# An attention and two feed-forward layers on one core: part of the first feed-forward block done inside the attention, in half units, with PSUM divided anew and a TensorE turn between the layers

## The chip, the cores and the metric

The kernel runs on one core of a Trainium2 chip. A core has TensorE (PE in the rows; PEld is its weight load), VectorE (DVE), ScalarE (ACT), GpSimd (POOL), SyncE (SP, which only issues transfers here) and 16 DMA engines. The metric is the device time of one execution in microseconds; smaller is better.

## The reference

Inputs are float32. Three layers follow each other:

```python
B, H, S, D = 2, 8, 576, 64                      # attention
q_rot, k_rot = (rotate(q), rotate(k))           # rotary position coding
scores = scale * np.matmul(q_rot, k_rot.transpose(0, 1, 3, 2))
scores = scores - np.max(scores, axis=-1, keepdims=True)
attn = np.exp(scores)
attn = attn / (np.sum(attn, axis=-1, keepdims=True) + 1e-09)
x = np.matmul(attn, v)                          # then to [1152 tokens, 512]

p = domain_probs / (domain_probs.sum(-1, keepdims=True) + 1e-09)
for e in range(4):                              # first feed-forward layer
    h = np.maximum(x @ w1[e], 0.0)              # 512 -> 1024
    out += p[:, e:e + 1] * (h @ w2[e])          # 1024 -> 512

h = out @ w_in                                  # second layer, 512 -> 2048
g = np.maximum(0.01 * h, h)
return g @ w_out                                # 2048 -> 512
```

## The kernel before

**Precision.** Each matmul operand is split into a rounded part and a rest ("hi" and "lo"), and three products (hi·lo, hi·hi, lo·hi) are summed in PSUM. For the weights POOL makes hi (L480) and lo (L484); for the hidden values ACT makes hi from PSUM (L531) and DVE lo (L535).

**Attention.** The 16 heads are worked on in pairs: pairs p = 0 to 3 belong to the first batch of 576 tokens, 4 to 7 to the second. For each pair x (q and k with their rotated partners) is loaded, rope is done by multiplications and an addition (L192, L195), hi and lo are made, and the halves are stacked into stk by transfers. A pair has nine score tiles: eight of 128 queries of one head (s, L275, four matmuls of 288 columns) and one for the 64 left queries of both heads. Each goes through DVE's maximum (L292), ACT's exponential (L302), transposes on PE (t, L348 and L354), hi on ACT (L373) and lo on DVE (L377). Two groups of queries (c = 0 with 320, c = 1 with 256) then give four sums over v (o, L430, in v_sum), whose two halves are added by ACT and DVE (L395, L400), and are multiplied by the reciprocals of the row sums, which two groups of transposes (rb, L332) spread over the partitions. x_out writes hi and lo into xT, the input of the next layer, turned, with tokens along the free axis. The PSUM of this part: ps_s two tiles of two banks, ps_t three banks for t and rb, ps_o one bank for o.

**Feed-forward.** xT has three blocks of tokens (512, 384, 256), xT0 to xT2. Block 0 holds tokens of the first batch only. The hidden columns are cut into 12 units of 512: units 0 to 7 are the four experts, two each, units 8 to 11 the second layer. For each unit u and block b stage 1 makes four tiles ph (L524, 12 matmuls each, relu or the leaky form on the way out), stage 2 one tile py (L430, 12 matmuls) for every 128 tokens, which DVE adds to acc (L567 to L574). Weights are transferred and split one unit ahead. The second layer's weights come as 64-bit values whose conversion (L495 to L513) uses DVE, POOL and ACT. Stage 1 of unit 0 on block 0 ("fill") is planned into the end of the attention, three matmuls at a time, and its weights are split there too.

**The turn between the layers.** After unit 7 acc, with tokens on the partitions, becomes the xT of the second layer. DVE transposes 32x32 blocks of an acc tile (L585), a transfer writes the tile of 256 KB to a DRAM buffer td (L590), four strided transfers read it back turned into xs (L599), ACT makes hi (L602) and DVE lo (L606). There are nine tiles.

**Order.** Nothing is ordered at run time. Plan is a list scheduler that runs when the program is built: each task has an engine or several to choose from, a length, what it comes after, and a rank; the task that can start earliest, and of those the one with the smallest rank, is put next on its engine. RANK and MORE hold the rank offsets of the attention's tasks, MORE what a second choice of engine adds. Ring stands for the rotation of a pool's buffers: a new tile comes after the users of the tile whose buffer it gets. There are two plans, one for the attention and one for the feed-forward part. On the chip each engine runs its list in order.

Of the kernel before, what the change touches and what calls it, by code (L numbers as in the profile page):

```python
# [20 lines left out]
P = 128  # L21
# [5 lines left out]
FU = 512  # L27
WARM = 22

RANK = {"tab_q": 1616.7, "zero": 1714.1, "load_x1": 1343.2, "load_x0": 2035.5, "rope01": 1752.5, "rope11": 2011.1, "rope21": 2017.5, "rope00": 2016.3,  # L30
        "rope10": 2000.0, "rope20": 1286.4, "x_hi1": 1338.5, "x_lo1": 1797.8, "x_hi0": 1168.4, "x_lo0": 1247.5, "stack1": 1313.2, "stack0": 1342.0,
        "diag": 1829.6, "load_v": 2038.3, "v_hi": 1678.4, "v_lo": 1951.8, "first_diag": 1240.7, "first_q": 1338.7, "scores": 1176.7, "max": 1822.3,
        "exp": 2029.1, "turn": 1666.7, "t_hi": 1805.0, "t_lo": 1825.5, "v_sum": 2012.8, "v_copy": 1150.2, "v_add": 1277.5, "r_add": 1843.8, "r_inv":
        1936.1, "r_rows": 1790.6, "r_wide": 1760.7, "x_mul": 1431.7, "x_out_hi": 2033.4, "x_out_lo": 2016.2, "load_w": 1702.3, "split_w": 1791.5,
        "fill0": 1333.5, "fill1": 2064.3, "fill2": 2004.3, "fill3": 1161.5, "fill_hi": 2024.3, "fill_lo": 1243.1}
# [14 lines left out]
LAG = {"PE": 0.2, "ACT": 0.16, "DVE": 0.19, "POOL": 0.1, "SP": 0.65, "DMA": 2.2}  # L50


class Plan:
# [17 lines left out]
    def order(self):  # L71
# [10 lines left out]
        while len(order) < len(self.tasks):  # L82
            best = None
            for e, items in ready.items():
# [7 lines left out]
            _, _, i, us = min((x for x in ready[e] if x[0] <= t), key=lambda x: x[0] if e == "DMA" else x[1:3])  # L92
# [35 lines left out]
def attention_then_two_ffns(ctx, tc, xqk, vp, rope, dprob, w1, w2, w_in, w_out, out):  # L128
# [8 lines left out]
    w1a_p = ctx.enter_context(tc.tile_pool(name="w1a", bufs=1))  # L137
    ha_p = ctx.enter_context(tc.tile_pool(name="ha", bufs=1))
# [25 lines left out]
    x_p, hl_p, stk_p, v_p, vs_p = opened("x", 2), opened("hl", 1), opened("stk", 2), opened("v", 1), opened("vs", 2)  # L164
    p_p, pl_p, st_p, pt_p = opened("p", 2), opened("pl", 2), opened("st", 4), opened("pt", 1)
    xo_p, tab_p, sm_p = opened("xo", 1), opened("tab", 1), opened("sm", 2)
    ps_s, ps_t, ps_o = (opened(n, b, space=PSUM) for n, b in (("ps_s", 2), ("ps_t", 3), ("ps_o", 1)))
# [159 lines left out]
    def r_rows(p, c):  # L327


        RB[p, c] = ps_t.tile([P, 3 - c, P], F32, tag="t", name=f"rb{p}_{c}")  # L330
        for j in range(2):
            pe.transpose(RB[p, c][:, j], RW[p, c][:, j].rearrange("p h d -> p (h d)"), ident)  # L332
        if c == 0:
            pe.transpose(RB[p, c][:, 2], SM[p][:, 4:5].to_broadcast([P, P]), ident)

    def t_turn(p, i, u):
# [6 lines left out]
        if i < KT:  # L343
            t = ps_t.tile([P, 3, P], F32, tag="t", name=f"t{p}_{i}_{u}")
# [4 lines left out]
        else:  # L349
            t = ps_t.tile([P, KT + 1, KR], F32, tag="t", name=f"t{p}_{i}_{u}")  # L350
# [28 lines left out]
    def v_sum(p, h, c):  # L379
        pt, vs = PT[p, c], VS[p]  # L380
        o = PO[p, h, c] = ps_o.tile([P, sum(k for _, k in RUNS[c])], F32, tag="o", name=f"o{p}_{h}_{c}")
# [54 lines left out]
    SEQ = [(u, b) for u in range(NU) for b in range(3)]  # L436
# [150 lines left out]
    def turn_out(blk, i):  # L587
        t = BLOCKS[blk][0] // P + i
        td = td_p.tile([P, DM], F32, tag="td", name=f"td{t}")
        sp.dma_start(td, TURN[blk, i])  # L590
        TURN[blk, i] = td

    def turn_in(blk, i, q):
        t = BLOCKS[blk][0] // P + i
        if q == 0:
            TURN["x", blk, i] = xs_p.tile([P, NC, P], F32, tag="xs", name=f"xs{t}")

        src = TURN[blk, i].rearrange("(a j) (c q i) -> q j c a i", a=4, c=NC, q=4)
        sp.dma_start(TURN["x", blk, i][32 * q:32 * q + 32].rearrange("j c (a i) -> j c a i", a=4), src[q])  # L599

    def turn_hi(blk, i):
        act.activation(xT[blk][:, 0, :, i * P:(i + 1) * P], TURN["x", blk, i], AF.Copy)  # L602

    def turn_lo(blk, i):
        s = slice(i * P, (i + 1) * P)
        dve.tensor_tensor(out=xT[blk][:, 1, :, s], in0=TURN["x", blk, i], in1=f32(xT[blk][:, 0, :, s]), op=ALU.subtract)  # L606


    with tc.manual_schedule():

        t = ps_o.tile([P, P], F32, tag="o", name="warm")
        for _ in range(WARM):
# [3 lines left out]
        rings = {k: Ring(v) for k, v in {"xk": 2, "xq": 2, "hl": 1, "stk": 2, "v": 1, "vs": 2, "p": 2, "pl": 2, "s": 2, "t": 3,  # L616
                                         "pt0": 1, "pt1": 1, "o": 1, "xf0": 1, "xf1": 1, "sm": 2, "rw": 2}.items()}
# [15 lines left out]
        def transfer(kind, n, fn, kb, after):  # L633
            return dma(fn, kb, after, n + RANK[kind], 0.48 if "load" in kind else 0.65)
# [14 lines left out]
        for p in range(NP_ALL):  # L649
# [52 lines left out]
            muls = []  # L702
            sm_t, sm_w = fresh("sm")
            for n in range(n0, n0 + PER):
# [21 lines left out]
                for u in ([1, 2] if h else [0]) if big else [0, 1]:  # L726
                    t_t, t_w = fresh("t")
# [3 lines left out]
                    for k in range(1 if big else 2):  # L731
# [3 lines left out]
                        rings["t"].use(t_t, lo)  # L735
                        for g in [0, 1] if big and u == 1 else [u // (1 + big)]:
                            written.setdefault((g, c), []).append(lo)
                if (i, h) in ((1, 1), (KT - 1, 1)):
# [3 lines left out]
                    for g in range(2):  # L742
                        o_t, o_w = fresh("o")
# [6 lines left out]
                        rings["o"].use(o_t, adds[-1])  # L750
# [199 lines left out]
```

## Time and profile before

| | us |
|---|---|
| median of 3 runs (lowest, highest) | 810.25 (809.1, 812.9) |
| the profiled execution | 808.0 |
| its span | 806.1 |
| PE busy | 756.7 (94%) |
| PEld busy | 666.8 (83%) |
| DVE busy | 429.3 (53%) |
| POOL busy | 379.0 (47%) |
| ACT busy | 293.1 (36%) |

The span is the time from the first to the last instruction of the profiled execution. The busy times are sums over a program with parts of very different character, the attention up to about 190 us, the feed-forward layers behind it, with the turn at about 570 to 618 us, so what bounds the kernel is read part by part.

### The profile page before, as it was taken

The page shows a single profiled execution, that of the slowest core. Times are in us where ns is not written, and L with a number is a line of the kernel's source. Part 1 is how long each engine was busy: PE and PEld are TensorE (multiplying, and loading weights), DVE is VectorE, ACT ScalarE, POOL GpSimd, SP SyncE. Part 2 cuts the span into 40 slices and gives each one's busy share as a digit, 9 for nine tenths or more (in the row PEclk, how much of TensorE's full clock was granted, in tenths as well). Part 3 has the DMA queues.
Part 4 walks back from the last instruction along what each step waited for, and adds up shares of the span by engine and source line. Part 5 has one row for each costly group of instructions (what it writes and reads, how often), then busy time and mean ns, then how long its engine had stood idle before and what let it go on. Part 6 is the DMA issues. An engine that isn't in the chain of part 4 may idle for free.

```text
span 806.1 us, 11011 instructions
## 1 busy us (share of the span) xinstructions
PE 756.7 (94%) x4160; PEld 666.8 (83%) x4160; DVE 429.3 (53%) x691; ACT 293.1 (36%) x666; POOL 379.0 (47%) x395
## 2 busy tenths in 40 slices
PE   6888888899999999999999999999956999999998
PEld 6777777788988888888888888889745889888897
DVE  7879999884132222222224222378785388773222
ACT  3878888772011011101112011224354445552221
POOL 7777777625903321333313333145374368673221
PEclk9999999999999999999999999999978999999999
DMA  7566665540401101111003111032774031000011
GB/s 227 140 180 173 160 168 156 121 178 27 157 26 53 48 14 45 52 53 53 27 27 104 53 53 32 22 105 79 168 210 92 1 104 53 1 1 1 0 53 66
DMA packets 47348, 66.13 MB, mean 82 GB/s; under 512 B 22848, under 2 KB 24640, under 8 KB 47296
## 3 DMA queue, kind: packets, MB, share of 16 engines
q1 hardware_dynamic: 47296, 65.44, 28.0%
q8 instruction: 33, 0.54, 0.3%
q14 instruction: 19, 0.16, 0.1%
HBM read 48.32 MB, written 4.72 MB: 66 GB/s over the span
## 4 chain that ended last, share of the span: by engine, by line
PE 79%; DVE 12%; ACT 3%; DMA 2%; issue 1%; POOL 1%; SPq 1%; DVEq 0%; ACTq 0%; POOLq 0%
PE ph L524 36%; PE py L430 33%; PE s L275 4%; PE o L430 4%; DVE pt L377 3%; DVE nm L292 3%; PE t L348 1%; DVE bd L288 1%; DVE xf L400 1%; ACT p L302 1%; ACT pt L373 1%; DMA raw<-in_w_in_dram 1%; DMA tab<-in_rope_dram 1%; DMA xs<-td 1%; SPq L599 1%
## 5 line engine op out<-in xcount | busy, mean ns | idle before, releaser
L524 PE MATMUL ph<-xT,w 128*128 128x256 f32 (+2 forms) x1728 | 308.7, 337 | 9.9 <-DVE xT L606 9.9
L524 PEld LDWEIGHTS ph<-xT,w 128*128 128x128 f32 x1728 | 281.0, 190 | 35.1 <-DVE xT L606 10.3
L430 PE MATMUL py<-w,h 128*128 128x512 f32 (+1 forms) x1308 | 302.7, 389 | 6.6 <-ACT h L547 5.5
L430 PEld LDWEIGHTS py<-w,h 128*128 128x128 f32 x1308 | 243.5, 188 | 57.4 <-ACT h L547 6.2
L531 ACT ACTIVATE h<-ph 128x512 fp32r<-128x512 f32 (+2 forms) x96 | 46.8, 492 | 305.3 <-PE ph L524 289.1
L480 POOL TENSOR_SCALAR w<-raw 128x512 fp32r<-128x512 f32 x64 | 40.0, 648 | 187.4 <-PE py L430 99.2
L535 DVE SCALAR_TENSOR_TENSOR h<-ph,h 128x512 fp32r<-128x512 f32 (+2 forms) x96 | 53.1, 557 | 127.7 <-ACT h L531 127.7
L570 DVE SCALAR_TENSOR_TENSOR acc<-py,prob,acc 128x512 f32<-128x512 f32 x63 | 47.1, 747 | 94.4 <-PE py L430 94.4
L549 POOL TENSOR_TENSOR h<-g,h 128x512 fp32r<-128x512 f32 (+2 forms) x48 | 51.5, 1073 | 77.3 <-ACT h L547 48.3
L484 POOL TENSOR_TENSOR w<-raw,w 128x512 fp32r<-128x512 f32 x64 | 81.5, 1299 | 0.0
L513 POOL TENSOR_TENSOR w<-t,w 128x512 fp32r<-128x512 f32 x32 | 44.1, 1392 | 48.8 <-ACT w L510 48.8
L275 PE MATMUL s<-stk 128*128 128x288 f32 x288 | 54.4, 323 | 12.4 <-ACT p L302 8.3
L504 POOL TENSOR_TENSOR t<-t,r 128x512 int32<-128x512 int32 x32 | 45.0, 1407 | 34.9 <-DVE t L497 24.1
L377 DVE TENSOR_TENSOR pt<-t,pt 128x384 fp32r<-128x384 f32 (+2 forms) x128 | 58.1, 489 | 2.3 <-ACT pt L373 1.2
L275 PEld LDWEIGHTS s<-stk 128*128 128x128 f32 x288 | 43.3, 201 | 16.5 <-ACT p L302 11.2
L373 ACT ACTIVATE pt<-t 128x384 fp32r<-128x384 f32 (+2 forms) x128 | 52.3, 440 | 11.5 <-PE t L348 10.0
L292 DVE TENSOR_REDUCE nm<-s 128x1 f32<-128x576 f32 x72 | 53.8, 753 | 4.7 <-PE s L275 3.9
L302 ACT ACTIVATE p<-s,nm 128x576 f32<-128x576 f32 x72 | 53.3, 741 | 5.2 <-DVE nm L292 4.7
L430 PE MATMUL o<-pt,vs 128*128 128x320 f32 (+1 forms) x256 | 46.3, 306 | 6.0 <-DVE xf L400 5.7
L348 PE MATMUL t<-ident,p 128*128 128x128 f32 x288 | 44.6, 283 | 3.1 <-DVE pt L377 2.5
L545 DVE TENSOR_TENSOR g<-ph,g 128x512 f32<-128x512 f32 (+2 forms) x48 | 26.5, 553 | 37.2 <-ACT g L543 37.0
L543 ACT ACTIVATE g<-ph 128x512 f32<-128x512 f32 (+2 forms) x48 | 23.4, 488 | 62.1 <-PE ph L524 59.4
(80 smaller groups left out, 644.3 us busy)
## 6 DMA issues: line engine op xcount, KB each, us to landing
raw<-in_w_dram SPq DMA_DIRECT2D x32, 512.0 KB, 3.7
raw<-in_w_in_dram SPq DMA_DIRECT2D x16, 512.0 KB, 4.1
raw<-in_w_out_dram SPq DMA_DIRECT2D x16, 512.0 KB, 3.7
x<-in_xqk_dram SPq DMA_DIRECT2D x14, 576.0 KB, 5.3
stk<-hl SPq DMA_DIRECT2D x28, 288.0 KB, 4.8
stk<-hl SPq DMA_DIRECT2D x28, 144.0 KB, 2.5
v<-in_vp_dram SPq DMA_DIRECT2D x8, 288.0 KB, 4.7
td<-tr SPq DMA_DIRECT2D x9, 256.0 KB, 2.5
```

Of the source, the lines that this page charges most:

```text
L275: pe.matmul(sc[:, c, :HS], lhsT=l, rhs=r[:, c * HS:(c + 1) * HS], start=(k == 0), stop=(k == len(ops) - 1))
L292: dve.tensor_reduce(out=NM[n], in_=SC[n][:, :, :HS], axis=AX.XY, op=ALU.max, negate=True)
L302: act.activation(PP[p, i][:, h].rearrange("p (c k) -> p c k", c=2), SC[n][:, :, :HS], AF.Exp, bias=NM[n], accum_out=SM[p][:, col:col + 1])
L348: pe.transpose(t[:, j], flat[:, b * P:(b + 1) * P], ident)
L373: act.activation(hi, src, AF.Copy)
L377: dve.tensor_tensor(out=lo, in0=src, in1=f32(hi), op=ALU.subtract)
L430: pe.matmul(ps, lhsT=l, rhs=r, start=(k == 0), stop=(k == len(ops) - 1))
L484: pool.tensor_tensor(out=w[:, 1], in0=raw, in1=f32(w[:, 0]), op=ALU.subtract)
L524: pe.matmul(ps, lhsT=w[:, c, l, fs], rhs=x[:, r, c], start=(c, k) == (0, 0), stop=(c, k) == (NC - 1, 2))
L535: dve.scalar_tensor_tensor(out=lo, in0=ps, scalar=0.0, in1=f32(hi), op0=ALU.max, op1=ALU.subtract)
L549: pool.tensor_tensor(out=lo, in0=g, in1=f32(hi), op=ALU.subtract)
L570: dve.scalar_tensor_tensor(out=acc, in0=ps, scalar=prob[:, t, e:e + 1], in1=acc, op0=ALU.mult, op1=ALU.add)
```

## The change

**Half units in the attention.** Block 0 of units 0 to 2 is taken out of the feed-forward order (`SEQ`) and done inside the attention's plan, after block 0 of xT is complete, that is, after pairs 0 to 3. Each unit is cut into two half units v of 256 hidden columns: two transfers of 512 KB (half_load), four hi splits on POOL or ACT and four lo splits on POOL, two tiles hp of 12 matmuls with their relu on ACT and DVE, and four tiles hy of six matmuls that DVE adds to acc. Units 0 to 2 still run on blocks 1 and 2 in the second plan, and transfer and split their weights again. The fill is gone. The normalisation of the domain probabilities moves into the attention's plan.

**PSUM.** ps_t and ps_o become ps_a and ps_b, two banks each (rings ta and tb). In pairs 0 to 3 the t, rb and o tiles alternate between them; in pairs 4 to 7 all of them use ta, and the half units use tb.

**Turn.** PE transposes each acc tile in four pieces into a ps_h tile, and ACT and DVE make hi and lo from PSUM. The DRAM buffer, its 45 transfers, and the pools td and xs are gone.

**Tables and pools.** RANK has two columns, for tasks before pair 4 and from it on, with new values. Rope tasks may go to DVE besides POOL. x has one ring of three instead of two of two, pl and rw one buffer instead of two. The first transfers are in another order.

```diff
-    ps_s, ps_t, ps_o = (opened(n, b, space=PSUM) for n, b in (("ps_s", 2), ("ps_t", 3), ("ps_o", 1)))
+    ps_s, ps_a, ps_b = (opened(n, 2, space=PSUM) for n in ("ps_s", "ps_a", "ps_b"))
...
-    SEQ = [(u, b) for u in range(NU) for b in range(3)]
+    SEQ = [(u, b) for u in range(NU) for b in range(u < AHEAD, 3)]
...
-        TURN[blk, i] = g_p.tile([P, DM], F32, tag="g", name=f"tr{t}")
-        dve.transpose(TURN[blk, i], ACC[t])
...
-        sp.dma_start(td, TURN[blk, i])
...
-        sp.dma_start(TURN["x", blk, i][32 * q:32 * q + 32].rearrange("j c (a i) -> j c a i", a=4), src[q])
+        TURN[blk, i] = ps_h.tile([P, NC, P], F32, tag="h", name=f"tr{t}")
+        for c in range(NC):
+            pe.transpose(TURN[blk, i][:, c], ACC[t][:, c * P:(c + 1) * P], ident)
...
+    def half_lo(v, which, j):
+        hi, lo, raw = half_parts(v, which, j)
+        pool.tensor_tensor(out=lo, in0=raw, in1=f32(hi), op=ALU.subtract)
+
+    def half_1(v, f, c):
+        if (v, f) not in HP:
+            HP[v, f] = ps_b.tile([P, 512], F32, tag="t", name=f"hp{v}_{f}")
+        w, x = HW[v, 0], xT[0]
+        for k, (l, r) in enumerate(((0, 1), (0, 0), (1, 0))):
+            pe.matmul(HP[v, f], lhsT=w[:, c, l, f * P:(f + 1) * P], rhs=x[:, r, c], start=(c, k) == (0, 0), stop=(c, k) == (NC - 1, 2))
...
+    def half_2(v, i):
+        ps = HY[v, i] = ps_b.tile([P, DM], F32, tag="t", name=f"hy{v}_{i}")
...
+        def fresh_bank(*what):
+
+            k = BANK[what] = banks[0] % 2 if what[1] < NPAIR else 0
+            banks[0] += 1
+            ring = ("ta", "tb")[k]
+            return (ring, *fresh(ring))
...
+                    need = [t] if c else parts[0][1] + x_done + b_w
+                    t = task("half_1", 4 * v + f, lambda e, v=v, f=f, c=c: half_1(v, f, c), [("PE", 0.69)], need)
...
+        weights(0, 0, -3)
         weights(0, 1, -2)
         weights(1, 0, 0)
...
+                    t = add(lambda e, b=b, i=i: turn(b, i), [("PE", 0.45, 0)], [a] + tr_w, k + 1.4)
...
+                    hi = add(lambda e, b=b, i=i: turn_hi(b, i), [("ACT", 0.5, 0)], [t] + first[u, b], k - 1)
+                    lo = add(lambda e, b=b, i=i: turn_lo(b, i), [("DVE", 0.6, 0)], [hi], k - 1)
```

PE at the start of pair 5, before: s are score tiles, t transposes of the exponentials.

```order
L275 MATMUL s48_1741<-stk5_1459 128x288 x4
L348 MATMUL t5_0_1_1751<-ident_67,p5_0_1692 128x128 x3
L275 MATMUL s49_1759<-stk5_1459 128x288 x4
L354 MATMUL t5_4_0_1766<-ident_67,p5_4_1738 128x64 x4
L355 MATMUL t5_4_0_1766<-ident_67,p5_4_1738 64x64
L275 MATMUL s50_1781<-stk5_1459 128x288 x4
```

Score tiles and transposes of pair 5 stand alone here.

PE at the same place after; hy1_1 and hy1_2 are tiles of the second stage of half unit 1.

```order
L371 MATMUL t5_0_1_1902<-ident_64,p5_0_1769 128x128 x3
L293 MATMUL s48_1912<-stk5_1521 128x288 x4
L453 MATMUL hy1_1_1919<-hw1_1_1779,hx1_1817 128x512 x6
L371 MATMUL t5_0_2_1933<-ident_64,p5_0_1769 128x128 x3
L377 MATMUL t5_4_0_1940<-ident_64,p5_4_1927 128x64 x4
L378 MATMUL t5_4_0_1940<-ident_64,p5_4_1927 64x64
L293 MATMUL s49_1948<-stk5_1521 128x288 x4
L453 MATMUL hy1_2_1956<-hw1_1_1779,hx1_1817 128x512 x6
```

Between one score tile and the next now stands a piece of six matmuls of a half unit.

POOL at the end of the attention, after: xT tiles are the attention's last output, w0_0 the first-stage weights of unit 0 for blocks 1 and 2.

```order
L251 TENSOR_SCALAR xT2_73<-xf7_1_2965 128x192
L448 TENSOR_TENSOR xT1_72<-xf7_1_2965,xT1_72 128x64
L448 TENSOR_TENSOR xT2_73<-xf7_1_2965,xT2_73 128x192
L503 TENSOR_SCALAR w0_0_3072<-raw0_0_0_3056 128x512 x2
L507 TENSOR_TENSOR w0_0_3072<-raw0_0_0_3056,w0_0_3072 128x512 x2
L503 TENSOR_SCALAR w0_0_3072<-raw0_0_1_3058 128x512 x2
L507 TENSOR_TENSOR w0_0_3072<-raw0_0_1_3058,w0_0_3072 128x512 x2
```

Before, the split of w0_0 stood among the rope and v tasks of pair 7; now it stands behind the last output of pair 7.

PE at the same place after; hy5 is the last half unit's second stage, ph0_1_0 the first tile of the second plan:

```order
L350 MATMUL rb7_1_2968<-ident_64,rw7_1_2867 128x128 x2
L453 MATMUL hy5_0_2972<-hw1_5_2898,hx5_2938 128x512 x6
L453 MATMUL hy5_1_2981<-hw1_5_2898,hx5_2938 128x512 x6
L453 MATMUL hy5_2_2993<-hw1_5_2898,hx5_2938 128x512 x6
L453 MATMUL hy5_3_3001<-hw1_5_2898,hx5_2938 128x512 x6
L547 MATMUL ph0_1_0_3086<-xT1_72,w0_0_3072 128x384 x12
```

Four hy tiles now stand between pair 7's last transposes and the first matmul that reads w0_0.

PE at the turn, before; py7 belongs to the last unit of the first layer, ph8 and py8 to the first unit of the second.

```order
L430 MATMUL py7_2_0_0_5447<-w1_7_4749,h7_2_5291 128x512 x12
L430 MATMUL py7_2_1_0_5473<-w1_7_4749,h7_2_5291 128x512 x12
L524 MATMUL ph8_0_0_5538<-xT0_74,w0_8_4938 128x512 x12
L524 MATMUL ph8_0_1_5569<-xT0_74,w0_8_4938 128x512 x12
L524 MATMUL ph8_0_2_5589<-xT0_74,w0_8_4938 128x512 x12
L524 MATMUL ph8_0_3_5617<-xT0_74,w0_8_4938 128x512 x12
L430 MATMUL py8_0_0_0_5680<-w1_8_5124,h8_0_5537 128x512 x12
L524 MATMUL ph8_1_0_5701<-xT1_75,w0_8_4938 128x384 x12
```

Unit 8 follows unit 7 here, block by block.

The same place after; tr7 and tr8 are the last two of the nine turned tiles.

```order
L547 MATMUL ph8_0_1_5576<-xT0_71,w0_8_5057 128x512 x12
L453 MATMUL py7_2_0_0_5604<-w1_7_4868,h7_2_5427 128x512 x12
L453 MATMUL py7_2_1_0_5626<-w1_7_4868,h7_2_5427 128x512 x12
L608 MATMUL tr7_5645<-ident_64,acc7_3391 128x128 x4
L547 MATMUL ph8_1_0_5655<-xT1_72,w0_8_5057 128x384 x12
L547 MATMUL ph8_0_2_5681<-xT0_71,w0_8_5057 128x512 x12
L608 MATMUL tr8_5704<-ident_64,acc8_3407 128x128 x4
L547 MATMUL ph8_1_1_5711<-xT1_72,w0_8_5057 128x384 x12
L547 MATMUL ph8_0_3_5734<-xT0_71,w0_8_5057 128x512 x12
L547 MATMUL ph8_1_2_5760<-xT1_72,w0_8_5057 128x384 x12
L547 MATMUL ph8_2_0_5789<-xT2_73,w0_8_5057 128x256 x12
L547 MATMUL ph8_1_3_5806<-xT1_72,w0_8_5057 128x384 x12
```

The first two tiles of unit 8 moved ahead of the last two py tiles of unit 7, and tiles of blocks 0, 1 and 2 of unit 8 now alternate.

## Rows read from the trace of the kernel before

**Rows 1.** Windows (start:end, length, busy time (instructions) per engine, PE clock, DMA share, GB/s).

```profile
98.00:118.00 20.00, 17.59 (x134) 15.95 (x133) 18.80 (x39) 17.00 (x47) 15.43 (x18) 1.00 0.61 164
138.00:160.00 22.00, 17.40 (x122) 15.98 (x121) 19.68 (x37) 16.40 (x45) 15.33 (x22) 0.92 0.56 147
582.70:618.00 35.30, 18.81 (x61) 13.94 (x62) 28.27 (x32) 17.75 (x31) 21.59 (x15) 0.76 0.54 142
```

**Rows 2.** PE timeline of pair 4's start: start, length, line, tile, count.

```profile
99.85 0.85 PE L430 MATMUL o<-pt,vs 128*128 128x320 f32 x4 [1.15 <-DVE xf L400]
...
101.41 1.21 PE L275 MATMUL s<-stk 128*128 128x288 f32 x8
102.46 0.49 PE L348 MATMUL t<-ident,p 128*128 128x128 f32 x3
102.78 0.38 PE L332 MATMUL rb<-ident,rw 128*128 128x128 f32 x2
...
103.25 0.73 PE L430 MATMUL o<-pt,vs 128*128 128x256 f32 x4
...
104.53 1.23 PE L275 MATMUL s<-hl,bd 128*128 128x288 f32 x8
...
121.37 1.21 PE L275 MATMUL s<-stk 128*128 128x288 f32 x8
```

**Rows 3.** PE timeline of the attention's end.

```profile
189.72 21.78 PE L524 MATMUL ph<-xT,w 128*128 128x512 f32 x129
```

**Rows 4.** Chain that ended last: startup transfer, feed-forward pieces, turn, end (start, length).

```profile
2.58 5.18 DMA tab<-in_rope_dram
...
230.57 10.88 PE ph L524 x48
241.45 5.44 PE py L430 x24
...
280.10 10.88 PE ph L524 x48
...
592.61 13.59 PE ph L524 x48
...
615.89 2.07 PE py L430 x4
...
788.98 13.79 PE py L430 x72
```

**Rows 5.** Waits from 526 to 622 us: total, times, longest.

```profile
PE ph L524 <- DVE xT L606: 9.9, 1, 9.9
```

**Rows 6.** Groups of instructions by form: busy and mean ns | idle before.

```profile
L484 POOL TENSOR_TENSOR w<-raw,w 128x512 fp32r<-128x512 f32 x64 | 81.5, 1299 | 0.0
...
L570 DVE SCALAR_TENSOR_TENSOR acc<-py,prob,acc 128x512 f32<-128x512 f32 x63 | 47.1, 747 | 94.4 <-PE py L430 94.4
...
L480 POOL TENSOR_SCALAR w<-raw 128x512 fp32r<-128x512 f32 x64 | 40.0, 648 | 187.4 <-PE py L430 99.2 <-PE ph L524 88.2
...
L535 DVE SCALAR_TENSOR_TENSOR h<-ph,h 128x512 fp32r<-128x512 f32 x32 | 22.1, 691 | 57.0 <-ACT h L531 57.0
...
L531 ACT ACTIVATE h<-ph 128x512 fp32r<-128x512 f32 x32 | 19.2, 598 | 108.6 <-PE ph L524 108.5
...
L216 DVE TENSOR_TENSOR hl<-x,hl 128x576 fp32r<-128x576 f32 x9 | 8.8, 998 | 0.4
```

**Rows 7.** Timeline in pair 6: one o and one t tile, from PE to last reader.

```profile
162.16 0.85 PE L430 MATMUL o<-pt,vs 128*128 128x320 f32 x4
...
164.40 0.49 DVE L400 TENSOR_TENSOR xf<-o,xf 64x320 f32<-64x320 f32 x1 [0.77 <-ACT xf L395]
164.80 0.49 PE L348 MATMUL t<-ident,p 128*128 128x128 f32 x3
...
167.19 0.56 DVE L377 TENSOR_TENSOR pt<-t,pt 128x384 fp32r<-128x384 f32 x1
```

More of the change, by code (lines that the diff above doesn't have):

```diff
@@ L27 @@
 FU = 512
+AHEAD = 3
+FH = FU // 2
 WARM = 22
[L30 to L35, printed above, removed]
@@ L46, with late, rank_of @@
 BLOCKS = [(0, 512), (512, 384), (896, 256)]
-LAG = {"PE": 0.2, "ACT": 0.16, "DVE": 0.19, "POOL": 0.1, "SP": 0.65, "DMA": 2.2}
+LAG = {"PE": 0.2, "ACT": 0.16, "DVE": 0.19, "POOL": 0.12, "SP": 0.65, "DMA": 2.2}
+def late(n):
+    return n >= NPAIR * (2 * KT + 1)
+def rank_of(kind, n):
+    return n + RANK[kind][late(n)]
 class Plan:
@@ L83, in order @@
             best = None
-            for e, items in ready.items():
+            for e in LAG:
+                items = ready.get(e, [])
                 items[:] = [x for x in items if x[2] not in done]
@@ L334, in r_rows, with bank @@
             pe.transpose(RB[p, c][:, 2], SM[p][:, 4:5].to_broadcast([P, P]), ident)
+    BANK = {}
+    def bank(*what):
+        return (ps_a, ps_b)[BANK[what]]
     def t_turn(p, i, u):
@@ L380, in v_sum @@
         pt, vs = PT[p, c], VS[p]
-        o = PO[p, h, c] = ps_o.tile([P, sum(k for _, k in RUNS[c])], F32, tag="o", name=f"o{p}_{h}_{c}")
+        o = PO[p, h, c] = bank("o", p, h, c).tile([P, sum(k for _, k in RUNS[c])], F32, tag="t", name=f"o{p}_{h}_{c}")
         ops = []
@@ new lines, in attention_then_two_ffns, with half_load, half_parts @@
+    HW, HX, HP, HY = ({} for _ in range(4))
+    def half_load(v, which):
+        e, q = divmod(v, 4)
+        cols = slice(q * FH, (q + 1) * FH)
+        src = (w2[e][cols, :] if which else w1[e][:, cols]).rearrange("(c p) f -> p c f", p=P)
+        raw = RAW["half", v, which] = hr_p.tile([P, 2 * FU], F32, tag="raw", name=f"hraw{v}_{which}")
+        sp.dma_start(raw.rearrange("p (c f) -> p c f", c=src.shape[1]), src)
+    def half_parts(v, which, j):
+        if (v, which) not in HW:
+            shape = [P, 2, 2, FU] if which else [P, NC, 2, FH]
+            HW[v, which] = hw_p.tile(shape, F32R, tag=f"hw{which}", name=f"hw{which}_{v}")
+        raw = RAW["half", v, which].rearrange("p (c f) -> p c f", c=2 if which else NC)
+        cs = slice(j, j + 1) if which else slice(2 * j, 2 * j + 2)
+        w = HW[v, which][:, cs]
+        return w[:, :, 0], w[:, :, 1], raw[:, cs]
@@ new lines, in half_relu @@
+    def half_relu(v, f, part):
+        if v not in HX:
+            HX[v] = hh_p.tile([P, 2, FH // P, 512], F32R, tag="hx", name=f"hx{v}")
+        hi, lo = HX[v][:, 0, f], HX[v][:, 1, f]
+        if part == 0:
+            act.activation(hi, HP[v, f], AF.Relu)
+        else:
+            dve.scalar_tensor_tensor(out=lo, in0=HP[v, f], scalar=0.0, in1=f32(hi), op0=ALU.max, op1=ALU.subtract)
+    def half_2(v, i):
+        ps = HY[v, i] = ps_b.tile([P, DM], F32, tag="t", name=f"hy{v}_{i}")
+        h, w, ts_ = HX[v], HW[v, 1], slice(i * P, (i + 1) * P)
+        ops = []
+        for f in range(FH // P):
+            ops += [(h[:, 0, f, ts_], w[:, f, 1]), (h[:, 0, f, ts_], w[:, f, 0]), (h[:, 1, f, ts_], w[:, f, 0])]
+        products(ps, ops)
@@ new lines, in attention_then_two_ffns @@
+                        rings[o_r].use(o_t, adds[-1])
+                    of = [exps[x, y] for x in ((2, 3) if c else (0, 1, KT)) for y in range(2) if (x, y) in exps]
+                    a1 = task("r_add", n, lambda e, p=p, c=c: r_add(e, p, c), [("DVE", 0.1), ("ACT", 0.2)], of)
+                    a2 = task("r_inv", n, lambda e, p=p, c=c: r_inv(p, c), [("DVE", 0.13)], [a1])
+                    rw_t, rw_w = fresh("rw")
+                    aw = task("r_wide", n, lambda e, p=p, c=c: r_wide(e, p, c), one(256, "ACT", "POOL"), [a2] + rw_w)
@@ L848, in attention_then_two_ffns @@
             first[u, b] = []
-            for f in range(FU // P if k else 0):
+            for f in range(FU // P):
                 p_t, p_w = fresh("ph")
```

233 lines of the change are left out of this document (117 added, 116 removed).

## The prediction

> **What bounds the kernel now.** The windows come first, since the share of busy time averages over unlike parts. In the attention [rows 1] a pair takes 20 us, from one pair's first score matmul at 101.41 to the next's at 121.37 [rows 2]. In such a stretch DVE is busy 18.80 us, PE 17.59, ACT 17.00, POOL 15.43: nobody is free, and DVE is nearest to the bound. But PE's busy time counts overlapping ends of matmuls. Its own work in a pair is read from start to start [rows 2]: eight score matmuls take 1.05 us (101.41 to 102.46), and a pair has five such groups, 5.3; three transposes take 0.32 (102.46 to 102.78), fourteen sets make 4.5; rb takes 0.47 (102.78 to 103.25); two sums of 320 columns take 1.56 each (99.85 to 101.41) and two of 256 take 1.28 each (103.25 to 104.53), 5.7. That is 15.9 of 20 us. Pairs 4 to 7 run from 101.41 to 189.72, where the long row of ph matmuls begins [rows 3]. That row has 129 of the 144 matmuls of its stage; the other 15, some 3.4 us at 10.88/48 = 0.227 each [rows 4], lie inside the attention. So the four pairs take 88.3 - 3.4 = 84.9 us, of which PE needs 4 x 15.9 = 63.6; it idles for **21.3 us**.
>
> In the feed-forward part PE is the bound. The chain that ended last [rows 4] is ph and py alone, and one unit repeats every 280.10 - 230.57 = 49.53 us. From 230.57 eleven more units and two py tiles (5.44) would end at 780.8; PE ends at 788.98 + 13.79 = 802.8. **The turn therefore loses 22.0 us.** 9.9 of them are one wait of ph for DVE's xT [rows 5]; then 48 matmuls take 13.59 us instead of 10.88 [rows 4], 2.7 more; and from 606.2 to 615.9, 9.7 us, the chain leaves PE for the leaky steps of the first tiles. In this stretch the granted clock averages 0.76 [rows 1], below the full 2.4 GHz of 98 to 118 us.
>
> The execution is then 101.4 (start and four pairs) + 63.6 + 21.3 (four pairs) + 594.4 (twelve units) + 22.0 (turn) + 3.3 (from 802.8 to the end of the span), which is 806.0 against 806.1.
>
> **The half units.** They move work, they don't save any: a half unit is 24 + 24 matmuls of 512 columns, 10.9 us at 0.227, and six make 65.4. That is what three units lose on block 0, 3 x (10.88 + 10.92). What may be saved is PE's idle time: in pairs 4 to 7 PE now has 63.6 + 65.4 = 129.0 us of work, and the order shows six-matmul pieces between score tiles. The others' load there stays below that. DVE: 4 x 18.8 = 75.2, twelve relu rests of 0.69 and 24 accumulations of 0.75 [rows 6] make 26, and some six rope operations at about 1.0 (nearest row: its subtraction of the same size, 0.998) replace others; about 105. ACT: 68 + 12 x 0.60 and some hi splits, 80. POOL: 61.7 + 24 x 1.30 + some 15 x 0.65, at most 103, less the ropes it gives to DVE. So PE bounds this stage. Its idle time there lies between 0 and the 21.3 of before; I take **8**, nearer to zero, since PE had no gaps in the units, where independent matmuls are at hand as they are now [rows 4], but the last half unit and pair 7 have little left to fill with. The weights of units 0 to 2 are loaded twice, 6 MB more in 137 us, 44 GB/s; attention's own 164 GB/s [rows 1] is stretched from 80 to 137 us, so the sum stays near its present rate. This costs nothing unless the queue holds up a stk transfer.
>
> **PSUM.** t, rb and o had four banks, now two in pairs 4 to 7. A pair uses 14 + 2 + 4 = 20 of them. A bank is held from PE's start to DVE's last read: 2.73 us for an o (162.16 to 164.89), 2.95 for a slow t (164.80 to 167.75) [rows 7]; most t are shorter, some 1.5 to 2, and I estimate a mean of 2.3. Two banks then carry 80 x 2.3 / 2 = 92 us of holds, under 129. No cost beyond the 8. In pairs 0 to 3 o no longer has one bank alone, which ends waits such as the 1.15 ahead of 99.85 [rows 2]; but ropes on DVE load the engine that is busiest there, a few us over four pairs, and the first q and the new order of the transfers put the second half of the rope table behind two more issues (it set the start: 2.58 to 7.76 [rows 4]). Together I take **+1.5** (from -3, if only the waits go, to +4.5).
>
> **From attention to feed-forward.** w0_0 was split during pair 7; now its eight POOL operations, 4 x 0.65 + 4 x 1.30 = 7.8 us [rows 6], stand behind pair 7's last output. That output, DVE's product and three small POOL operations, I estimate at 1.7 us (each well below POOL's 0.65 to 1.30 for 512 columns); 9.5 in all; PE has four hy tiles of 1.365, 5.5 us, as cover. The difference, **4.0**, is a stall; 0 if the last outputs come early, 7.8 if the cover ends before POOL starts. All units' later weights follow behind, but a unit gives POOL 49.5 us (less in the first three, 27.7, against 15.6 of splits).
>
> **The turn.** 36 transposes at 0.32/3 = 0.107 make **3.9 us** on PE, where there were none. DVE's block transposes, 45 transfers and their latencies go. The Trainium skill (VectorE: DVE Perf Modes, The three transpose paths) gives TensorE 390 ns for a 128x128 transpose, which would make this about 14 us; the transposes of this trace, at 0.107 apiece in a row, don't agree with it.
>
> What comes next after the 9.9: xT of block 0 is ready earlier, as its tiles can be turned between py tiles, and the order puts ph8 tiles ahead of the last py7 tiles. The leaky chain (ACT, DVE, ACT, POOL) is unchanged, but three ph8 tiles of other blocks now stand between the last ph8 tile of block 0 and py8, about 5.6 us. I take **3** of stall, from 1 to the 12.4 (9.7 + 2.7) that is left if only the first wait goes.
>
> **The sum.** 101.4 + 63.6 + 594.4 + 3.9 + 3.3 = 766.6; + 8 + 1.5 + 4 + 3 = 783.1 of span. The profiled execution took 1.9 us more than its span, and the median of the runs lies 2.25 above it: **787 us**, 23 less than 810.25.
>
> **Rivals.**
> *The mixed stage keeps attention's gaps.* The chain maximum, exponential, transpose, hi, lo, sum is as long as before, and each engine runs its list in order, so that PE may stand at a t whose exponential is late while a ready hy is behind it. For it: PE idles 0.7 to 1.2 us at such points now. Against it: the pieces lie between them. All 21.3 instead of 8: 801.
> *The turn keeps its second wait.* The conversions of the second layer's weights load DVE (28.27 of 35.3 us busy) and POOL (21.59) [rows 1] in the same stretch, so the leaky steps may queue behind them as now. 12.4 instead of 3: 797. Both rivals together: 810, no change.
> *Two banks too few (slower).* The hold grows when ACT's and DVE's reads queue behind the half units' relu and accumulations. Four pairs need 40 times the hold: from 3.4 us on this exceeds 137 and decides; at 4.0 (160 us) the gain is gone; at 4.5 the stage takes 180, 43 more: 830. For it: single holds of 2.73 and 2.95 exist already [rows 7] with DVE 94% busy. Against it: DVE's load falls to 105 of 137.
> *The clock (slower).* Where PE starts and stops, in 582.7 to 618, the granted clock averaged 0.76, and 48 matmuls took 13.59 for 10.88, 25% more; in 138 to 160 it averaged 0.92, in 98 to 118, with gaps as well, 1.00 [rows 1, 4]. If the mixed stage ran at the first of these, its 129 us would cost 32 more: 819.
> The Trainium skill (TensorE: Matmul & The Clock Gate, A second HAM failure mode: psum-queue depth-cycling) says that 512-column matmuls which cycle through PSUM banks can idle often enough to make the clock swing; two banks in tb would be such a cycle. The 0.76 agrees, the 1.00 in attention, with banks cycling too, doesn't.
>
> **How the numbers follow.** Forecast 787: 0.61, its own range 776 to 797 by the bounds of its four unknown terms, not all at one end. Gaps kept, 801: 0.14. Second wait kept, 797: 0.10. Both, 810: 0.04. Banks, 830: 0.07. Clock, 819: 0.04. The range from 776 to 803 holds the first three cases but for the forecast's own edges, about 0.8. Faster by over 0.5% (about what a measurement of this kernel tells from no change; below 806.2) are the first three, 0.85; within it 0.04; slower 0.11.
>
> **What would show it.** In the profile after: pair 4's first score at about 103; PE without gaps over 1 us from there to about 240, clock near 1.00; the wait of ph0_1_0 for POOL's w0_0 about 4 us; the wait for the turn gone, and 48 ph8 matmuls of 512 columns at 10.9; PE's end at about 780. Wrong would be: waits of t or s for DVE's pt that fill the mixed stage (banks), a clock below 0.9 there, or a wait of py8 for leaky steps of 5 us or more.

## The result and the profile after

The changed kernel takes 789.42 us (median of 4 runs, 788.45 to 791.62) against 809.67 us before; the ratio is 0.9747, with a 95% interval of 0.9711 to 0.9782. A second set of runs gave 788.29 us and 0.9735 (0.9709 to 0.9760). The forecast was 787, in a range of 776 to 803. The profiled execution has a span of 786.9 us, 19.2 less than before.

Windows of the changed kernel (columns as in [rows 1]): PE busy, PEld, DVE, ACT, POOL, granted clock, DMA share, GB/s.

```profile
100.00:120.00 20.00, 17.64 (x124) 15.13 (x122) 18.81 (x42) 16.65 (x44) 13.43 (x17) 1.00 0.40 104
120.00:140.00 20.00, 20.00 (x123) 17.59 (x122) 16.07 (x32) 12.04 (x31) 10.73 (x13) 1.00 0.62 165
...
118.00:240.00 122.00, 122.00 (x756) 107.38 (x757) 92.88 (x175) 73.48 (x186) 63.92 (x80) 1.00 0.46 132
```

Where a pair had PE busy 17.59 of 20 us before [rows 1], PE is now busy all of 122 us, at the full clock, and DVE, ACT and POOL have room. (Busy time counts the overlapping ends of matmuls; what PE stands still for is listed as waits below.) The PE timeline shows where the half units begin; pair 4's first score is at 108.75, the first hp tile at 118.36:

```profile
108.75 0.79 PE L293 MATMUL s<-stk 128*128 128x288 f32 x4
...
118.36 1.67 PE L650 MATMUL hp<-xT,hw 128*128 128x512 f32 x6
```

The waits of PE that are listed from 100 to 246 us (total, times, longest); those behind 108.75 are the 1.0 and one 0.4 of s, 1.4 us, all before 118:

```profile
PE t L371 <- DVE pt L400: 1.0, 1, 1.0
PE s L293 <- ACT p L320: 0.8, 2, 0.4
PE t L371 <- DVE xf L432: 0.4, 1, 0.4
```

The PE timeline at the end of the attention (start, length, line, tile, count) shows the last hy tiles and the first ph tiles of block 1, which wait 1.20 and 0.44 us for POOL's split of w0_0:

```profile
239.87 5.72 PE L453 MATMUL hy<-hw,hx 128*128 128x512 f32 x24
245.43 2.06 PE L547 MATMUL ph<-xT,w 128*128 128x384 f32 x8
248.69 0.79 PE L547 MATMUL ph<-xT,w 128*128 128x384 f32 x3 [1.20 <-POOL w L507]
249.92 12.31 PE L547 MATMUL ph<-xT,w 128*128 128x384 f32 x84 [0.44 <-POOL w L507]
```

At the turn the wait of 9.9 us [rows 5] is gone. Window, chain of waits and waits of PE:

```profile
580.00:620.00 40.00, 38.37 (x201) 33.46 (x200) 33.49 (x39) 22.43 (x43) 31.03 (x23) 1.00 0.32 95
```

```profile
545.95 0.44 PE tr L608 x4
...
551.24 0.87 PE tr L608 x8
...
769.96 13.79 PE py L453 x72
```

```profile
PE ph L547 <- DVE g L568: 1.4, 1, 1.4
PE tr L608 <- DVE acc L593: 0.3, 1, 0.3
```

The clock there is 1.00 instead of 0.76 [rows 1], four transposes take 0.44 us, and PE ends at 769.96 + 13.79 = 783.75.

Not everything is faster. The first maximum (DVE, one per score tile) of each pair, in us, read from the DVE timelines; "changed, again" is the second profile of the same kernel, and "before, again" that of the kernel before with the new turn alone (an experiment below), whose attention is that of before:

| kernel | p0 | p1 | p2 | p3 | p4 | p5 | p6 | p7 |
|---|---|---|---|---|---|---|---|---|
| before | 16.4 | 43.0 | 62.7 | 82.6 | 102.6 | 122.6 | 142.7 | 164.9 |
| before, again | 17.7 | 44.3 | 64.0 | 83.9 | 103.9 | 123.8 | 143.9 | 167.0 |
| changed | 18.2 | 46.9 | 67.5 | 86.4 | 110.2 | 137.2 | 173.6 | 199.3 |
| changed, again | 17.1 | 43.4 | 62.8 | 81.7 | 105.6 | 134.1 | 170.5 | 196.1 |

The first batch ends later than before: pair 4 starts 1.7 to 7.6 us late, by which two profiles are compared. In both profiles of the changed kernel pair 3 takes 23.8 or 23.9 us instead of 20.0.

### The profile page after: what moved, and what is told of

Read it like the earlier page. It is cut to its first block, busy times and chain, and to the rows that moved or that the text cites. A ratio compares the mean times of both kernels' runs of the same rounds, so it can differ in the third digit from the quotient of the medians.

```text
span 786.9 us, 11039 instructions
## 1 busy us (share of the span) xinstructions
PE 756.7 (96%) x4196; PEld 667.1 (85%) x4196; DVE 434.4 (55%) x705; ACT 299.8 (38%) x673; POOL 404.0 (51%) x425
## 3 DMA queue, kind: packets, MB, share of 16 engines
q1 hardware_dynamic: 31792, 67.01, 28.5%
## 4 chain that ended last, share of the span: by engine, by line
PE 85%; DVE 6%; ACT 4%; POOL 2%; issue 2%; DMA 1%; SPq 0%; ACTq 0%; DVEq 0%; POOLq 0%
PE py L453 33%; PE ph L547 31%; PE s L293 5%; PE o L453 4%; PE hp L650 4%; PE hy L453 4%; PE t L371 3%; ACT p L320 1%; DVE pt L400 1%; DVE nm L310 1%; ACT pt L396 1%; DMA tab<-in_rope_dram 1%; DVE t L518 1%; ACT hl L249 1%; POOL w L507 0%
## 5 line engine op out<-in xcount | busy, mean ns | idle before, releaser
L547 PE MATMUL ph<-xT,w 128*128 128x256 f32 (+2 forms) x1584 | 274.4, 331 | 3.2 <-POOL w L507 1.6
L547 PEld LDWEIGHTS ph<-xT,w 128*128 128x128 f32 x1584 | 252.1, 189 | 23.0 <-POOL w L507 2.3
L453 PE MATMUL py<-w,h 128*128 128x512 f32 (+1 forms) x1164 | 267.9, 388 | 0.0
L453 PEld LDWEIGHTS py<-w,h 128*128 128x128 f32 x1164 | 215.8, 188 | 43.4
L554 ACT ACTIVATE h<-ph 128x384 fp32r<-128x384 f32 (+2 forms) x84 | 40.0, 476 | 254.9 <-PE ph L547 254.9
L558 DVE SCALAR_TENSOR_TENSOR h<-ph,h 128x384 fp32r<-128x384 f32 (+2 forms) x84 | 45.1, 537 | 111.8 <-ACT h L554 111.8
L593 DVE SCALAR_TENSOR_TENSOR acc<-py,prob,acc 128x512 f32<-128x512 f32 x55 | 41.2, 749 | 85.4 <-PE py L453 85.4
L371 PE MATMUL t<-ident,p 128*128 128x128 f32 x288 | 46.9, 281 | 9.1 <-ACT p L320 3.8
L293 PEld LDWEIGHTS s<-stk 128*128 128x128 f32 x288 | 44.3, 203 | 12.7 <-ACT p L320 5.4
L371 PEld LDWEIGHTS t<-ident,p 128*128 128x128 f32 x288 | 34.9, 143 | 17.3 <-ACT p L320 5.0
```

The costliest lines, as they stand in the source:

```text
L293: pe.matmul(sc[:, c, :HS], lhsT=l, rhs=r[:, c * HS:(c + 1) * HS], start=(k == 0), stop=(k == len(ops) - 1))
L371: pe.transpose(t[:, j], flat[:, b * P:(b + 1) * P], ident)
L453: pe.matmul(ps, lhsT=l, rhs=r, start=(k == 0), stop=(k == len(ops) - 1))
L547: pe.matmul(ps, lhsT=w[:, c, l, fs], rhs=x[:, r, c], start=(c, k) == (0, 0), stop=(c, k) == (NC - 1, 2))
L558: dve.scalar_tensor_tensor(out=lo, in0=ps, scalar=0.0, in1=f32(hi), op0=ALU.max, op1=ALU.subtract)
```

## The experiments

Times are medians; the kernel before had 808.7 to 809.4 us beside them.

**The turn undone, and the turn alone.** The first run puts the turn through DRAM back into the changed kernel, the second puts the new turn into the kernel before. Each has the difference shown for the turn in the change, once backwards and once forwards, and nothing else.

> The changed kernel with the turn through DRAM put back (DVE block transposes, 45 transfers), all else as changed. Theory (the turn's loss of 22.0 us became about 3.9 of transposes and 3.4 of stall): the loss comes back, 789.4 + 22.0 - 7.3 = 804 us, with one wait of ph for DVE's xT of about 10 us. Rival (the new order of the second plan, not the transposes, took the stall away): 789 to 793.

> The kernel before with the turn by TensorE alone, attention untouched. Theory: 809.7 - 14.7 = 795 us, the wait of ph for xT gone, a stall of some 3 us for the leaky steps left. Rival (the second wait of 9.7 us stays, since the leaky steps queue behind the weights' conversions): 809.7 - 9.9 + 3.9 = 804.

Measured: 806.94 (ratio to before 0.9969, 0.9947 to 0.9991) and 794.15 (0.9808, 0.9780 to 0.9837). The times of both theories hold, the first somewhat exceeded; the wait of about 10 us of ph for xT that the first named does not, it is 4.6. PE's waits from 526 to 640 us, first with the turn through DRAM put back:

```profile
PE py L453 <- ACT h L570: 12.1, 2, 7.6
PE ph L547 <- DVE xT L629: 4.6, 1, 4.6
...
```

and with the TensorE turn alone in the kernel before:

```profile
PE ph L524 <- DVE g L545: 2.5, 1, 2.5
PE tr L585 <- DVE acc L570: 0.2, 1, 0.2
```

The new order of the second plan doesn't save the old turn: its stall moves from ph to py. So **the turn alone gains 15.3 us** (809.4 - 794.2), three quarters of the whole; all else alone gains 2.5 (809.4 - 806.9).

**Fewer units ahead.**

```diff
-AHEAD = 3
+AHEAD = 1
```

and the same with 2.

> The changed kernel with one unit (two half units) done ahead instead of three. Theory (the gain is the idle time of TensorE in pairs 4 to 7, some 21 us, and one unit of 21.8 us already fits into it, but leaves DVE, about 90 us in that stage, and the chains as the bound): 790 to 796 us. Rival (every unit taken ahead gains the same 7 us): 803.

> Two units ahead instead of three. Theory (with 63.6 + 43.6 = 107 us TensorE is the bound already, the third unit only moves work): 788 to 791 us. Rival (7 us per unit): 796.

Measured: 816.95 and 803.81. Theory and rival both fall: a unit is worth 13 to 15 us, more than either said, and with one unit the kernel is slower than before (1.0086, 1.0064 to 1.0109). The trace of two units shows why. The half units run out at about 206 us, pair 7 goes on alone, and nothing covers the split of w0_0 behind it:

```profile
204.82 1.54 PE L453 MATMUL hy<-hw,hx 128*128 128x512 f32 x6
...
221.59 0.55 PE L371 MATMUL t<-ident,p 128*128 128x128 f32 x3 [0.72 <-DVE xf L423]
222.57 0.52 PE L371 MATMUL t<-ident,p 128*128 128x128 f32 x3 [0.43 <-DVE xf L432]
...
234.73 1.01 PE L547 MATMUL ph<-xT,w 128*128 128x384 f32 x2 [3.08 <-POOL w L503]
236.54 2.82 PE L547 MATMUL ph<-xT,w 128*128 128x384 f32 x6 [0.80 <-POOL w L507]
240.16 15.12 PE L547 MATMUL ph<-xT,w 128*128 128x384 f32 x88 [0.80 <-POOL w L507]
```

Here ph starts at 234.73. In the changed kernel's second profile, whose first pair ran alike, it starts at 242.25; less one unit's 21.8 us that would be 220.5. The 14.3 us between are about what the medians lie apart (803.8 - 789.4 = 14.4), and they arise behind the last half unit: up to pair 7 the two keep one pace (pairs 4 to 6 take 28.4, 36.4 and 25.7 us here, 28.5, 36.4 and 25.6 there), so it isn't that the rank table, made for three units, would fit two units badly. Part of them are waits such as those of t and the 3.08 at the end. The clock, 0.69 from 220 to 240 us, goes with slow first ph tiles, six matmuls in 2.82 us where later 88 take 15.12:

```profile
220.00:240.00 20.00, 13.29 (x55) 9.47 (x53) 6.01 (x14) 5.09 (x12) 8.34 (x13) 0.69 0.06 12
```

The expectation compared totals of work over the stage, when what counts is whether independent work is left at its end.

**The interleaving undone, with two banks and with four.** The half units wait for all eight pairs instead of the first block alone; the second run also lets pairs 4 to 7 use all four banks.

```diff
-                        if piece[0] == 0:
-                            x_done.append(lo)
+                        x_done.append(lo)
...
-            k = BANK[what] = banks[0] % 2 if what[1] < NPAIR else 0
+            k = BANK[what] = banks[0] % 2
```

> The changed kernel with the half units held back until all eight pairs are done: the same work, weights, tables and banks, only the interleaving undone, so that pairs 4 to 7 run alone on two banks and the six half units follow in a row. Theory (interleaving fills the 21 us that TensorE idles in pairs 4 to 7, and two banks bind once nothing lies between, 92 us of holds against 85; the 65 us of half units at the end hide the split of w0_0, 4 us less): 806 to 815 us. Rival (the tables made the gain, interleaving little): 788 to 793.

> As the run before, but t, rb and o of pairs 4 to 7 alternate over all four banks, as in pairs 0 to 3. Theory (two banks cost the unmixed pairs their holds, 80 x 2.3 / 2 = 92 us against some 80 to 85): 4 to 10 us below the run before. Rival (the banks don't matter even there): equal to it within 2 us.

Measured: 824.22 and 817.24, above the first range. The difference of 7.0 us is inside the 4 to 10 of the theory: two banks do bind once the pairs run alone. (In the profiles 5.2 us of the difference lie between pair 4's first maximum and the first hp tile.) PE's waits from 100 to 290 us, with two banks:

```profile
PE t L371 <- DVE pt L400: 7.4, 16, 1.0
PE t L371 <- DVE xf L432: 4.0, 6, 1.1
...
PE t L371 <- DVE xf L423: 2.9, 3, 1.5
...
```

and with four:

```profile
PE t L371 <- ACT p L320: 11.4, 10, 1.6
PE t L371 <- DVE xf L432: 4.2, 4, 1.5
...
```

The t tiles then wait for their exponentials instead of for the last reader of a bank. But the 35 us that undoing the interleaving costs are not all its worth. From pair 4's first maximum to the first hp tile the second run takes 207.0 - 108.3 = 98.7 us, where the kernel before took 189.7 - 102.6 - 3.4 = 83.7 for the same pairs. A likely reason is the rank table's second column, made for interleaved pairs; no run shows it. The fairer comparison is the kernel before with the new turn, 794.15 (792.8 to 796.8), against the changed kernel's 789.42 and 788.29 (786.5 to 791.6 in both sets): **the interleaving with all that it brings (banks, tables, ropes on DVE) gains about 5 us, 4.7 to 5.9.**

**One bank.** Four pools of one bank each replace ps_a and ps_b; pairs 0 to 3 rotate over them as in the changed kernel, pairs 4 to 7 use one.

```diff
-            k = BANK[what] = banks[0] % 2 if what[1] < NPAIR else 0
+            k = (0, 2, 1, 3)[banks[0] % 4] if what[1] < NPAIR else 0
```

> The changed kernel with one bank instead of two for t, rb and o in pairs 4 to 7, half units interleaved as before. By the estimate of the prediction (80 uses held 2.3 us each) one bank is held 184 us against 129 us of TensorE's work: 835 to 850 us, with many waits of t for DVE's pt. Rival (the holds are 1.6 us or less, or hide behind the pieces): 789 to 800.

Measured: 863.39, 74 us more than with two. The theory's direction holds; its size was too small, and the loss comes about in another way. Read tile by tile in the timelines, from PE's start to DVE's last read, the last 72 t and o tiles (four pairs' worth) hold their bank for 2.2 us on average here and for 2.0 in the changed kernel, both under the 2.3 that the prediction estimated. As long as there are half units, the one bank is not the bound: pair 5 takes 51.2 us (140.1 to 191.3), of which the bank is held for 35.8, while PE, with pieces of half units between, is busy for 49.0. But the last hy tile starts at 218.8, in the middle of pair 6, and from there to the first ph tile at 316.0 nothing is left to fill the waits. The bank is then held for 89 of 94 us (up to 313), PE's listed waits make 39.5 us, and the clock falls. Windows of pair 5, of the stretch behind the last half unit, and of a piece of it:

```profile
140.10:191.30 51.20, 49.01 (x267) 40.66 (x266) 32.52 (x55) 24.42 (x59) 29.09 (x35) 1.00 0.43 114
219.00:316.00 97.00, 55.12 (x231) 42.61 (x230) 30.81 (x63) 29.68 (x77) 6.51 (x17) 0.60 0.11 38
```

```profile
220.00:240.00 20.00, 11.49 (x49) 9.18 (x50) 6.68 (x16) 7.04 (x20) 0.01 (x1) 0.61 0.16 53
```

PE's waits from 100 to 290 us:

```profile
PE t L372 <- DVE pt L401: 17.6, 15, 1.5
PE t L378 <- DVE pt L401: 4.1, 5, 1.2
...
```

How much of the 74 us is the bank's and how much the clock's was not told apart. With two banks 80 x 2.0 / 2 = 80 us of holds stay under the stage's 129.

**What slows the first batch?** Five runs looked for it. They settle the part of the first pair; for pair 3 the trace has to be read beside them. First the changed kernel again, and one with more warming matmuls:

```diff
-WARM = 22
+WARM = 38
```

> The changed kernel once more, unchanged, beside the next three on the same chip: 787 to 792 us. Its profiled run before had TensorE at a granted clock of 0.50 from about 14 to 27 us and the first pair took 28.7 us from its first maximum to the second pair's; two kernels with the same attention were at 0.50 to about 21 us and took 26.3. If this differs from run to run, this profile may show either.

> The changed kernel with 38 instead of 22 warming matmul pairs, so that TensorE is busy to about 14.5 us instead of 9.1 and doesn't stand idle before the first scores (13.2). Theory (the idle time makes the clock fall, and the first pair pays 1 to 3 us for it): clock 1.00 from 12 to 40 us, first to second pair 25 to 26 us, the whole 1 to 4 us under the changed kernel, 786 to 788. Rival (DVE bounds the first pair, the clock costs nothing): the same 789.

Measured: 788.29 and 789.43; no difference. The first run differs from the profile above as the expectation allowed: the clock recovers at about 18 instead of 27 us. Windows of the changed kernel, then of its second run, then of the one with 38:

```profile
16.00:20.00 4.00, 3.17 (x14) 2.82 (x12) 3.12 (x5) 2.19 (x4) 4.00 (x6) 0.50 0.66 171
20.00:24.00 4.00, 3.13 (x14) 3.11 (x15) 1.00 (x3) 2.03 (x5) 3.69 (x7) 0.50 0.99 275
```

```profile
12.00:16.00 4.00, 2.47 (x9) 2.18 (x10) 3.51 (x6) 1.33 (x3) 2.08 (x2) 0.50 0.29 73
16.00:20.00 4.00, 2.30 (x11) 1.95 (x11) 2.61 (x4) 2.93 (x6) 3.77 (x8) 0.72 0.71 211
20.00:24.00 4.00, 3.70 (x36) 3.38 (x34) 3.12 (x4) 2.49 (x8) 3.92 (x4) 1.00 0.92 256
```

```profile
12.00:16.00 4.00, 1.68 (x10) 1.32 (x9) 3.88 (x9) 0.96 (x2) 1.32 (x2) 0.97 0.19 51
16.00:20.00 4.00, 2.13 (x9) 1.78 (x8) 3.06 (x5) 2.52 (x4) 3.92 (x6) 0.50 0.65 177
20.00:24.00 4.00, 3.45 (x15) 3.44 (x16) 1.15 (x2) 1.71 (x5) 3.77 (x6) 0.50 0.99 275
```

More warming only moves the stretch at 1.2 GHz (0.50) to a later place: the clock falls at 15.7 us all the same, with PE busy 1.68 us of the 4 around it. My theory of the warming falls. Pair 0 pays for the stretch: it takes 26.3 us where the clock recovers early, 28.7 and 30.0 where it doesn't. Eight of the profiles, with 22 warming pairs, have this first batch in the same order on every engine, and they agree: 26.2 or 26.3 us where the clock is back by 18.3 to 19.8 (four), 27.5 to 27.7 where it is back at about 24.3 (two), 28.6 or 28.7 at 27.0 (two).

Then the bank division of before in pairs 0 to 3 (t and rb on three banks, o on one; pools of one bank as above), rope on POOL alone, and the first transfers in the order of before (k and table first):

```diff
-            k = BANK[what] = banks[0] % 2 if what[1] < NPAIR else 0
+            if what[1] < NPAIR and what[0] == "o":
+                k = 3
+            else:
+                k = banks[0] % (3 if what[1] < NPAIR else 2)
```

```diff
...
-two(m, *(("POOL", "DVE") if p else ("POOL",))), need)
+two(m, "POOL"), need)
...
```

(the end of one of the three lines; in the other two DVE goes as a choice of pairs 1 to 7 in the same way)

```diff
+    if n < 1 and kind in ("load_x1", "load_x0"):
+        return n + (1343.2 if kind == "load_x1" else 1500.0)
```

> The changed kernel with the PSUM division of before in pairs 0 to 3 (t and rb on three banks, o on one), the new one from pair 4 on. Theory (the new division costs nothing in pairs 0 to 3; the fourth pair's 23.8 us has another cause): 788 to 791. Rival (the two and two alternating banks slow the first batch): 784 to 787.

> The changed kernel with the rope of pairs 1 to 7 on POOL alone, as before; DVE loses some 15 operations of about 1 us, nine of them ahead of pair 4. Theory (DVE, 18.4 to 18.8 us busy of 20 in the first batch, is slowed by them there): pair 4 begins 2 to 5 us earlier and the whole is 785 to 788. Rival (POOL's later x delays the stacks): 789 to 795.

> The changed kernel with the first transfers in the order of before (k, table, k, table, then q) in place of q first. Theory (first maximum at 17.1 to 18.2 us with q first, 16.4 before): 0 to 2 us faster than the changed kernel, 786 to 789. Rival (the order of the list that follows changes with it and costs more): 790 or more.

Measured: 806.46, 804.67 and 814.27: every one is 15 to 26 us slower. The last does start earlier (first maximum at 15.4), but pair 0 then takes 36.1 us, though only six transfers at the start were put in another order. The scheduler fills every list anew when one task moves, and the rank table was made for this one configuration, so these runs measure the misfit of the table together with the part that was undone. They show that neither ropes on DVE nor the new banks are a loss that can be taken back by itself. (The last two also make the tile xf at whichever of its halves is planned first; that changes no work.)

For pair 3 the trace of the changed kernel says more. Its stretch, from one first maximum to the next, and the rope operations that DVE does in it (count | busy, mean ns | idle before):

```profile
86.40:110.20 23.80, 20.50 (x149) 17.63 (x148) 23.28 (x47) 19.67 (x52) 18.14 (x21) 1.00 0.54 139
```

```profile
L210 DVE TENSOR_TENSOR x<-x,tab 128x576 f32<-128x576 f32 x1 | 1.9, 1855 | 0.0
...
L213 DVE TENSOR_TENSOR x<-x 128x576 f32<-128x576 f32 x2 | 1.9, 926 | 0.0
```

DVE is busy for 23.28 of 23.80 us and bounds the stretch. The three ropes, 3.7 us, are as much as it is longer by; in the kernel before DVE did none there. The plan also moved lo parts of t tiles into it, 20 instead of 16, from pair 2, which is 1 us shorter. With rope on POOL alone pair 3 takes 21.3 us, but pairs 1 and 2 take 25.8 and 25.1. So the trace points to DVE's added work as what makes pair 3 longer; that taking the ropes away would undo it, no run shows.

No kernel of these beat the changed one.

## Why the prediction was right

By its own terms, in the changed kernel's profile of 786.9 against the predicted span of 783.1:

| term | predicted | measured | from |
|---|---|---|---|
| pair 4's first score later than before | +1.5 | +7.3 (+2.7 in the second profile) | 108.75 (104.10) - 101.41 |
| PE idle while pairs 4 to 7 run | 8 | 7.7, of which 1.4 are waits | 245.43 - 108.75 - 129.0 |
| stall behind the attention | 4 | 1.6 | 1.20 + 0.44 |
| transposes of the turn | 3.9 | 4.0 | 9 x 0.44 |
| stall in the turn | 3 | 1.7 | 1.4 + 0.3 |
| the units themselves | 529.0 (594.4 - 65.4) | 531.0 | 783.75 - 245.43 - 1.6 - 4.0 - 1.7 |

**Right:** the turn. It was the largest part, its loss of 22 us was read from one unit's period, and both runs on the turn bear it out. The price of a transpose was taken from the trace, where 0.107 became 0.11; the Trainium skill's 390 ns (VectorE: DVE Perf Modes, The three transpose paths), which stands there for 128x128 of bf16, does not fit these rows of float32.

**Right in sum by luck:** the idle time in pairs 4 to 7. The 8 were to be gaps with the last half unit and pair 7. There PE waits for nothing; the waits from 108.75 to 245.43 are 1.4 us, all before 118, while pair 3 finishes and the half units still wait for its last output in xT. The gaps were filled better than forecast, but the work was dearer: the 288 matmuls of the half units came 0.240 us apart on average, start to start, where the sum took 0.227 from the units, which makes 3.9 us; the other 2.4 went to attention's own matmuls. One piece of a half unit and what follows it, 1.48 us for six:

```profile
121.46 1.64 PE L650 MATMUL hp<-xT,hw 128*128 128x512 f32 x6
122.94 0.82 PE L371 MATMUL t<-ident,p 128*128 128x128 f32 x6
```

Why they come further apart between other matmuls, no run shows.

**Mis-sized:** the start and first batch. The range of -3 to +4.5 holds the second profile's +2.7, not the first's +7.3. The step that failed is the one that weighed the first transfers and DVE's ropes alone and let the saved waits for o's bank pay for part of them. In its place the runs show two things. Pair 3, where DVE was busy for 23.28 of 23.80 us, grew by 3.8 and 3.9 in the two profiles. And the clock at the start, which the sum put at nothing, differs from execution to execution: it was at 0.50 for 13.6 us in the first profile (13.3 to 26.9), for 6.9 in the second and for 3.4 in the kernel before, and the first pair is 2.4 us longer in the first profile than in the second. Two stalls taken too high, 3.7 us together, hid most of it. The one behind the attention (4.0 against 1.6) took PE to wait for the whole split of w0_0; but eight ph matmuls ran from 245.43 on, while POOL was at the split from 242.52 to 249.9.

**The rivals.** Gaps kept (801) and the second wait kept (797) didn't happen: the waits at these places make 1.4 and 1.7 us. Two banks too few: a hold of 2.0 us is under the estimate of 2.3 and under the 3.4 from which it decides, so the rival stayed away; with one bank it came, but behind the last half unit only. The clock: the mixed stage ran at 1.00 from 118 to 240 us; in the second profile it began with 3.4 us at 0.50 (113.8 to 117.2) and then ran at 1.00 too. What the Trainium skill says of a swinging clock (TensorE: Matmul & The Clock Gate, A second HAM failure mode: psum-queue depth-cycling) doesn't come into force here: matmuls of 512 columns cycle through two banks for 122 us, but PE has no gaps between them. The 0.76 at the old turn, which the prediction took to agree with this, is no sign of it: that stretch holds one wait of 9.9 us for xT [rows 5].

**How little the interleaving brings in all.** The prediction's own terms make it 21.3 - 8 - 1.5 - 4 = 7.8 us beside the turn's 15. With the measured ones it is 21.3 - 7.7 - 7.3 - 1.6 = 4.7, what the medians of 794.2 and 789.4 say too; that the two agree so closely is luck, since the profiled executions of these kernels are about 8 us apart (spans of 795.1 and 786.9).

## What to carry to other kernels

Read the loss of a transition from the period around it, not from the longest wait in it: here one unit's 49.53 us showed 22 us lost where the longest wait was 9.9, and the simplest part of the change, transposes on the bound engine for 4 us, gained three quarters of the whole. When work is interleaved to fill an engine, count whether enough is left at the end of the stage, where the last dependent chain and the next stage's preparation need cover; one unit less cost 14 us there. And where a tuned table sets the order, taking one part back measures the misfit of the table too: compare against the other kernel that was tuned for itself.

## What the runs showed of the hardware

TensorE's granted clock fell to 0.50 (1.2 GHz) around the first scores, whether the engine had stood idle for 4 us before them (22 warming pairs; it fell at 13.3 and at 11.4 us) or for 0.7 and, between the first two, 1.6 us (38; at 15.7). How long it stayed there differed between executions of one and the same kernel, until 18.3 or 26.9 us, worth 2.4 us in the first pair. Filled gaps gave a steady 1.00 for 122 us; with one bank, where PE was busy 11.5 of 20 us, it was 0.61. Four 128x128 transposes of float32 in a row took 0.44 us. A PSUM bank was held for 2.0 us on average by a t or o tile that ACT and DVE read in turn, with PE shared by half units.
